# One LayerNorm group for token tiles 0 and 1, and a new task order ahead of the second FFN chunk

## The chip, the cores and the metric

The kernel runs on one core of one Trainium2 chip. The metric is the device time of one launch in microseconds (us), as the median of several runs. Its engines are TensorE (PE, whose weight loads have a row of their own, PEld), VectorE (DVE), ScalarE (ACT), GpSimd (POOL) and SyncE (SP), which issues nearly all the DMAs.

## The reference

One transformer block on 2048 tokens of width 512: linear attention with a softmax feature map, then a gated FFN, both with a LayerNorm that is modulated by a condition vector c. The shapes are in the comments.

```python
mod = (silu(c) @ w_mod)                 # 6 vectors of 512: sa, ca, ga, sb, cb, gb
h = layernorm(x) * (1 + ca) + sa        # 2048 x 512
q, k, v = h @ wqkv                      # 32 heads of 16
pq, pk = q @ w_phi, k @ w_phi           # per head, 16 x 16
phi = lambda p: concat(softmax(p), softmax(-p))   # 32 features per head
kv = phi(pk).T @ v;  z = sum over tokens of phi(pk)
o = (phi(pq) @ kv) / (phi(pq) @ z + 1e-6)
x = x + ga * (o @ wo)
h = layernorm(x) * (1 + cb) + sb
x = x + gb * ((sigmoid(h @ w_gate) * (h @ w_up)) @ w_down)   # F = 1376
```

## The kernel before

The 2048 tokens are 16 tiles of 128. The program is a graph of 1230 small tasks with names; the text ORDER lists them all in one line, and each task's instructions go to the queue of its engine in that order. A name may end in @A, @D or @P, which puts the task on ACT, DVE or POOL; without it the task goes to the first engine in its own list. Every engine works its queue strictly in order. Buffers of a class (eight PSUM banks, eight `xn` and so on) are given out along the same text. Nothing else sets the order.

The tasks, with their lines in the kernel before:

- `ld_*`: loads, issued by SP (L537 x, L545 half of the K weights, L542 a quarter of the modulation weights). `wqT*` (L669) are transposed loads of the Q weights.
- `c1 c2 c3` turn c into silu(c); `modc1.0` and `modc1.1` (L630) are the products with the modulation weights, `modc1c0` and `modc1c1` (L635 to L638) copy the results out, each for half of the four 128-wide slices of D.
- `tpw*` (PE, L661) transpose the K weights, `wTc*` (L664) copy them out, `fold1*` (L679) fold w_phi into them, `foldc1*` (L685) copy that out. `fold0*` does the same for Q.
- First LayerNorm, by groups of tiles (the list LG): `st1_t` (DVE, L702) statistics, `rs1_g` the reciprocal root (ACT L709 or POOL L712), `nmr1_g` (DVE, L718) minus mean times that, `xn1_t` (L727 ACT, L729 DVE, L731 POOL) the normalised tile, `tph` (PE, L744) its transpose, four tasks per group, and `hm1` (L751 ACT, L753 DVE and POOL), which copies out a transposed slice with the modulation. An hm1 of a group of two tiles is 256 wide, of one tile 128. Before, tiles 0 and 1 are groups of their own; the others are pairs.
- Keys of tile t: `Kt` (PE, L817, four matmuls of 512 columns, for tiles 0 to 7 in halves a and b), `et` (ACT, L776, exp of both signs), `nt` (DVE, L780, sums), `rt` (the reciprocal, DVE L798 or ACT L794 and L795), `phit` (L787, DVE or POOL). Values: `Vt` (PE, L821) and `vat` (ACT, L836, the copy). `kvt` (PE, L282) adds phi times v into two PSUM banks. Tile 11 is cut in four parts for this, tiles 13 to 15 in two.
- `kvz` and `kvn` (DVE, L299 and L294) copy the two finished sums out. Only then can any output begin.
- Queries: `Qt` (PE, L871), `qet`, `qnt`, `qphit.s` (L784), `pTt` (a transposing DMA, L874).
- Output of a tile: `num` (PE, L326), `rd` and `u` (DVE, L329 and L333, the division), `oT`, `out` (PE, L356), `x1` (DVE, L361), then the second LayerNorm (`st2`, `rs2`, `nmr2`, `xn2`, `xnT`, `mod`). `tsw` loads the table for tanh on ACT.
- FFN by chunks of 1, 1, 2, 4, 4 and 4 tiles: `g` and `u` (PE, L447), `tg` (ACT, L457), `hm` (DVE, L468), `y` (PE, L485), `fin` (DVE, L492), `st` (the store).
- `warm0` (six matmuls) and `warm1_0` to `warm1_11` (one each, PE, L600) multiply zeros from the last block of w_down. The load of that block's real rows, `ld_wd2`, waits for the last of them.

## Time and profile before

| | us |
|---|---|
| median of 3 runs | 203.33 |
| lowest, highest | 203.19, 203.52 |
| span of the profiled execution | 202.2 |
| PE busy in it | 194.4 (96%) |
| DVE busy | 160.6 (79%) |
| ACT busy | 105.3 (52%) |
| POOL busy | 104.2 (52%) |

The profiled execution's time is known only as this span, from its first to its last instruction. Busy shares are means over stages of very different kinds: the start until the first K, the stage of keys and values, and the long rest, in which the outputs and the FFN run. They are read stage by stage. A matmul's record in the trace is longer than the distance to the next, since matmuls are pipelined; prices are therefore taken from start to start.

### The profile page before, as it was taken

What the parts mean: (1) busy time and instruction counts of PE and PEld (TensorE: products, weight loads), DVE (VectorE), ACT (ScalarE), POOL (GpSimd) and SP (SyncE); (2) the same over time, 40 slices, a digit from 0 to 9 for tenths busy, and PEclk for the clock granted to TensorE, in tenths of its full rate; (3) what the DMA queues carried; (4) which work ended last, traced back from release to release, by engine and by line L of the source; (5) the groups of instructions that cost most, each with busy time, mean ns of one, the idle gap of its engine ahead of it and who ended that gap; (6) DMA issues with size and microseconds to landing.
All of it is one profiled execution on the core that took longest, in us unless ns stands there. A gap on an engine that the chain in (4) does not pass through costs nothing.

```text
span 202.2 us, 4128 instructions
## 1 busy us (share of the span) xinstructions
PE 194.4 (96%) x1447; PEld 106.2 (53%) x1471; DVE 160.6 (79%) x376; ACT 105.3 (52%) x250; POOL 104.2 (52%) x146
## 2 busy tenths in 40 slices
...
GB/s 169 329 262 239 289 232 111 114 71 261 396 254 77 133 109 51 82 39 108 117 79 80 53 79 85 100 104 52 26 26 81 2 78 54 28 5 26 28 54 57
DMA packets 49452, 22.92 MB, mean 113 GB/s; under 512 B 38065, under 2 KB 47634, under 8 KB 49426
## 3 DMA queue, kind: packets, MB, share of 16 engines
...
q8 instruction: 12, 0.20, 0.4%
...
HBM read 11.58 MB, written 2.10 MB: 68 GB/s over the span
## 4 chain that ended last, share of the span: by engine, by line
PE 70%; ACT 15%; DVE 8%; issue 2%; POOL 2%; DMA 1%; POOLq 0%; DVEq 0%
PE y_ps L485 19%; PE u_ps L447 18%; PE g_ps L447 18%; PE a_ps L356 5%; ACT h1T L751 3%; ACT e L776 3%; ACT qe L776 2%; PE num L326 2%; PE k_ps L817 2%; DVE qks L780 2%; ACT wqk_f L685 2%; PE v_ps L821 2%; DVE ks L780 1%; DMA x_sb<-in_A_x_dram 1%; DVE phi L787 1%
## 5 line engine op out<-in xcount | busy, mean ns | idle before, releaser
L457 ACT ACTIVATE tg<-g_ps 128x512 bf16<-128x512 f32 (+5 forms) x66 | 28.7, 455 | 66.8 <-PE g_ps L447 39.9
L468 DVE SCALAR_TENSOR_TENSOR wmod_sb<-tg,u_ps 128x512 bf16<-128x512 bf16 (+4 forms) x63 | 30.2, 491 | 18.0 <-ACT tg L457 11.5
L485 PE MATMUL y_ps<-wd_sb,wmod_sb 128*128 128x512 bf16 (+4 forms) x180 | 44.2, 366 | 0.2
L447 PEld LDWEIGHTS <-wg_sb 128*128 128x128 bf16 (+1 forms) x252 | 21.9, 99 | 16.1 <-issue 0.2
L447 PEld LDWEIGHTS <-wu_sb 128*128 128x128 bf16 (+1 forms) x252 | 21.7, 99 | 15.9 <-issue 0.3
L784 POOL TENSOR_TENSOR qphi<-qe,qks 128x512 bf16<-128x512 bf16 x24 | 25.1, 1064 | 4.1 <-DMA pT<-qphi 1.4
L485 PEld LDWEIGHTS <-wmod_sb 128*128 128x128 bf16 (+1 forms) x187 | 17.1, 98 | 16.0 <-issue 0.6
L447 PE MATMUL u_ps<-wT_sb,wu_sb 128*128 128x512 bf16 (+2 forms) x124 | 23.8, 322 | 0.1
L447 PE MATMUL g_ps<-wT_sb,wg_sb 128*128 128x512 bf16 (+2 forms) x122 | 23.0, 321 | 0.2
L447 PE MATMUL g_ps<-wqk_sb,wg_sb 128*128 128x128 bf16 (+4 forms) x127 | 19.9, 287 | 0.1
L447 PE MATMUL u_ps<-wqk_sb,wu_sb 128*128 128x128 bf16 (+4 forms) x127 | 19.8, 286 | 0.2
L780 DVE TENSOR_REDUCE ks<-e 128x64 f32<-128x1024 bf16 (+2 forms) x22 | 19.3, 904 | 0.2
L492 DVE TENSOR_TENSOR ot<-y_ps,x 128x512 bf16<-128x512 f32 (+2 forms) x17 | 11.1, 654 | 10.1 <-PE y_ps L485 10.1
L780 DVE TENSOR_REDUCE qks<-qe 128x64 bf16<-128x1024 bf16 x16 | 19.1, 1204 | 0.0
L376 POOL TENSOR_SCALAR ve<-mv 128x2 f32<-128x2 f32 (+1 forms) x8 | 1.8, 226 | 33.4 <-DVE mv L366 33.3
L776 ACT ACTIVATE e<-k_ps 128x512 bf16<-128x512 f32 (+2 forms) x44 | 18.3, 536 | 0.0
L776 ACT ACTIVATE qe<-q_ps 128x512 bf16<-128x512 f32 x32 | 17.1, 612 | 0.8 <-POOL phi L787 0.6
L787 POOL TENSOR_TENSOR phi<-e,kr 128x1024 bf16<-128x1024 bf16 (+2 forms) x10 | 14.9, 1501 | 2.5 <-DVE phi L787 1.2
L817 PE MATMUL k_ps<-wqk_f,h1T 128*128 128x512 bf16 x61 | 16.1, 379 | 0.1
L356 PE MATMUL a_ps<-wo_sb,oT 128*128 128x512 bf16 x60 | 15.9, 379 | 0.2
L871 PE MATMUL q_ps<-wqk_f,h1T 128*128 128x512 bf16 x61 | 15.7, 379 | 0.2
L821 PE MATMUL v_ps<-wv_sb,h1T 128*128 128x512 bf16 x61 | 15.3, 379 | 0.1
...
## 6 DMA issues: line engine op xcount, KB each, us to landing
...
```

The source lines that it names most:

```text
L356: pe.matmul(ap_[:], lhsT=oT[:, j, :], rhs=wo_sb[:, j, :], start=(j == 0), stop=(j == KT - 1))
L447: pe.matmul(ps[:fsz, 0:n], lhsT=w[:, j, ft * P:ft * P + fsz], rhs=h[:, j, 0:n], start=(j == 0), stop=(j == KT - 1))
L457: G.add(f"tg{k}.{ft}", {"ACT": 0.13 + n * 0.00083}, lambda e, tg=tg, g_ps=g_ps, fsz=fsz, n=n: act.activation(tg[:fsz, 0:n], g_ps[:fsz, 0:n ...
L468: dve.scalar_tensor_tensor(hm_all[:fsz, hm[k].slot, ft, 0:n], tg[:fsz, 0:n], 1.0, u_ps[:fsz, 0:n], op0=ALU.add, op1=ALU.mult)
L485: mm = pe.matmul(y[:, 0:c1 - c0], lhsT=hm_all[:fsz, hm[k].slot, ft, tl * P:(tl + 1) * P], rhs=wd_sb[:fsz, ft, c0:c1], start=(ft == 0), sto ...
L776: act.activation(ee[:, a:b, s].rearrange("p g f h -> p g (f h)"), kp[:, a * 64:b * 64].rearrange("p (g n) -> p g n", n=64), ACT.Exp, scale ...
L780: dve.tensor_reduce(ks[:, a:b].rearrange("p g s h -> p (g s) h"), ee[:, a:b].rearrange("p g s f h -> p (g s) h f"), axis=AX.X, op=ALU.add)
L784: engine(e).tensor_tensor(ph[:].rearrange("p (g s f h) -> p g s f h", s=2, f=DH, h=4)[:, :, s], ee[:, :, s], ks[:, :, 1 - s].unsqueeze(2). ...
L787: engine(e).tensor_tensor(ph[:, a * P:b * P].rearrange("p (g f h) -> p g f h", f=DH, h=4), ee[:, a:b].rearrange("p g s f h -> p (g s) f h" ...
L817: pe.matmul(kp[:], lhsT=h1T[:, j, t * P:(t + 1) * P], rhs=wqk_f[:, j, D:2 * D], start=(j == 0), stop=(j == KT - 1))
L821: pe.matmul(vp[:], lhsT=h1T[:, j, t * P:(t + 1) * P], rhs=wv_sb[:, j, :], start=(j == 0), stop=(j == KT - 1))
L871: pe.matmul(qp[:], lhsT=h1T[:, j, t * P:(t + 1) * P], rhs=wqk_f[:, j, 0:D], start=(j == 0), stop=(j == KT - 1))
```

## The change

The list LG is changed so that tiles 0 and 1 form one group, and TD (which groups are transposed by DMA) accordingly. Tile 0's `xn1` had been bound to DVE and now takes the common form, with an `nmr` of its own (list XP). The tasks rs1_1, nmr1_1 and the four tph and four hm1 of tile 1 alone are gone; the four hm1 of the group are 256 wide. Tasks of the first LayerNorm are now named by their group's first tile (rs1_8 is the group of tiles 8 and 9, before rs1_5). 1221 tasks are left.

ORDER is new up to the second FFN chunk, and some 45 tasks stand on other engines. From the second chunk on the order of the matmuls is the same. New switches come with it: HALF, QHALF, RPAIR are empty and ROWS and WPQ are 0, so that the code they guard makes no tasks. The tile `mone` is wider.

```diff
-LG = [[0], [1], [2, 3], [4, 5], [6, 7], [8, 9], [10, 11], [12, 13], [14, 15]]
-TD = [0, 0, 0, 0, 0, 0, 1, 1, 0]
+LG = [[0, 1], [2, 3], [4, 5], [6, 7], [8, 9], [10, 11], [12, 13], [14, 15]]
+TD = [0, 0, 0, 0, 0, 1, 1, 0]
...
+XP = [1, 2, 3, 4, 5, 6, 7, 8, 9, 10, 11, 12, 13, 14, 15, 0]
...
-        if g:
-            def f_nm(e, ts=ts):
-                for t in ts:
+        xp = [t for t in ts if t in XP]
+        if xp:
+            def f_nm(e, xp=xp):
+                for t in xp:
...
-            G.add(f"xn1_{t}", {"POOL": 0.69, "ACT": 0.73} if t else {"DVE": 0.3}, f_xn, r=[("rs1", g)] + ([("nmr1", g)] if t else []), w=[("xn1", t)],
+            G.add(f"xn1_{t}", {"POOL": 0.69, "ACT": 0.73, "DVE": 0.3} if t in XP else {"DVE": 0.3}, f_xn, r=[("rs1", g)] + ([("nmr1", g)] if t in XP else []), w=[("xn1", t)],
```

Two lines of ORDER in its new form, from the end of the keys stage; `warm1_8` to `warm1_11` had stood ahead of the first K:

```diff
+V13 warm1_8 warm1_9 Q3 r12.0 phi15.0@D phi12.0@D r15.4@A qn6.0 va13 kv12.0 kv13.0 kv13.4 va15 kv14.0 kv15.0 kvz0 kvn0 phi15.4 kv14.4 kv15.4 kvz1 kvn1 wo0 wo2
+wo3 qe3.0 qn3.0 qphi3.1@P qphi3.0@P Q7 qe7.0 num0a rd0a num0b rd0b Q15 num2b warm1_10 warm1_11 num1a num1b num4a num2a gwb grb ld_wu0 ld_wd ld_wg0 qphi6.0@P
```

The engines whose load moves, tile by tile:

- hm1 from DVE to ACT: 0.2, 6.0, 4.3, 8.0, 8.2, 14.1, 14.3 (14.x is the slice x of the group of tiles 14 and 15); from ACT to DVE: 2.1, 4.0, 6.3; of the two groups transposed by DMA, 10.1 from POOL to ACT, 12.1 from ACT to POOL, 12.0 from POOL to DVE.
- phi from DVE to POOL: 3, 4, 7, three quarters of 11 and a half of 13; from POOL to DVE: 6 and 8.
- r from DVE to ACT: 3, 6, 8 and a half of 14; from ACT to DVE: 4, 5, 9, 12.
- xn1_3 from ACT to POOL, xn1_0 from DVE to POOL, xn1_6 from POOL to DVE; rs1_8 from POOL to ACT; modc1c0, foldc02 and va2 from ACT to DVE.

Three places of the order, engine by engine. First ACT from the first reciprocal root (`rs_84`) to the first exp (`e`), before:

```order
L709 ACTIVATE ve_83<-mv_82,eps 128x1
L710 ACTIVATE rs_84<-ve_83 128x1
L727 ACTIVATE xn<-x_sb,nmr,rs_84 128x512
L664 COPY wT_sb<-tp_w 128x4x128 x4
L685 CAST wqk_f<-fold_ps 128x512 x3
L635 COPY modc<-modc_ps 128x2
L636 ACTIVATE modc<-modc_ps 128x2
L751 ACTIVATE h1T<-tp_h,modc 128x256
L751 ACTIVATE h1T<-tp_h,modc 128x128
L751 ACTIVATE h1T<-tp_h,modc 128x256
L751 ACTIVATE h1T<-tp_h,modc 128x128
L685 CAST wqk_f<-fold_ps 128x512
```

And the same place now:

```order
L740 ACTIVATE ve_83<-mv_82,eps 128x2
L741 ACTIVATE rs_84<-ve_83 128x2
L695 COPY wT_sb<-tp_w 128x4x128 x4
L716 CAST wqk_f<-fold_ps 128x512 x4
L783 ACTIVATE h1T<-tp_h,modc 128x256 x9
L810 ACTIVATE e<-k_ps 128x8x64 x2
```

The xn and the modc copies are gone from here, the wT copies come right behind the roots, and nine wide h1T stand in one run.

Second the loads that SP issues first, before:

```order
L537 DMA x_sb<-in_A_x_dram 128x2x512 x2
L545 DMA wqk_sb<-in_A_wqkv_dram 128x2x512
L537 DMA x_sb<-in_A_x_dram 128x2x512
L545 DMA wqk_sb<-in_A_wqkv_dram 128x2x512
L537 DMA x_sb<-in_A_x_dram 128x2x512
L542 DMA wmod_sb<-in_w_mod_dram 128x4x256 x2
L537 DMA x_sb<-in_A_x_dram 128x2x512
L542 DMA wmod_sb<-in_w_mod_dram 128x4x256 x2
L537 DMA x_sb<-in_A_x_dram 128x2x512
L669 DMA_TRANSPOSE wT_sb<-in_A_wqkv_dram 128x4x128
L537 DMA x_sb<-in_A_x_dram 128x4x512
L551 DMA wv_sb<-in_A_wqkv_dram 128x4x512
```

And now:

```order
L546 DMA x_sb<-in_A_x_dram 128x2x512 x3
L559 DMA wqk_sb<-in_A_wqkv_dram 128x2x512 x2
L546 DMA x_sb<-in_A_x_dram 128x2x512
L554 DMA wmod_sb<-in_w_mod_dram 128x4x256 x2
L546 DMA x_sb<-in_A_x_dram 128x2x512
L554 DMA wmod_sb<-in_w_mod_dram 128x4x256 x2
L546 DMA x_sb<-in_A_x_dram 128x2x512
L546 DMA x_sb<-in_A_x_dram 128x4x512
L565 DMA wv_sb<-in_A_wqkv_dram 128x4x512
L700 DMA_TRANSPOSE wT_sb<-in_A_wqkv_dram 128x4x128 x4
```

The first half of the K weights (`wqk_sb`) is now the fourth load instead of the third, tiles 0 and 1 come first (the rows don't tell tiles apart), and all transposed loads stand behind wv.

Third ACT at the end of the keys stage, from a full exp of a query (`qe`) to the next, before:

```order
L776 ACTIVATE qe<-q_ps 128x8x64 x2
L836 CAST vaug_110<-v_ps 128x32x16
L794 ACTIVATE ks<-ks 128x32
L795 ACTIVATE kr<-ks 128x32
L836 CAST vaug_113<-v_ps 128x32x16
L836 CAST vaug_111<-v_ps 128x32x16
L776 ACTIVATE qe<-q_ps 128x8x64 x4
```

And now:

```order
L877 CAST vaug_111<-v_ps 128x32x16
L877 CAST vaug_110<-v_ps 128x32x16
L810 ACTIVATE qe<-q_ps 128x8x64 x2
L833 ACTIVATE ks<-ks 128x32
L834 ACTIVATE kr<-ks 128x32
L877 CAST vaug_113<-v_ps 128x32x16
L877 CAST vaug_112<-v_ps 128x32x16
L810 ACTIVATE qe<-q_ps 128x8x64 x6
```

In both the last half reciprocal (`ks`, `kr`) is followed by two copies of values (`vaug`); now three more queries' exps come right behind, where before there were two.

More of the change, by code (lines that the diff above doesn't have):

```diff
@@ L35 @@
 DIRECT = [1, 0]
+HALF = []
+QHALF = []
+XP = [1, 2, 3, 4, 5, 6, 7, 8, 9, 10, 11, 12, 13, 14, 15, 0]
+RPAIR = []
+ROWS = 0
+WPQ = 0
 VSP = 4
@@ new lines @@
+rs1_6@P ld_wk0 warm1_6 tpw1 wTc1 tpw0 wTc0 ld_wk1 tpw3 wTc3 tpw2 wTc2 fold11 foldc11 fold13 foldc13 fold12 foldc12 tph0.0 fold10 foldc10 nmr1_2 xn1_2 xn1_3
+ld_x1a st1_5 c3 nmr1_6 xn1_7 st1_4 rs1_4@P ld_wm00a ld_wm00b modc1.0 tph0.2 modc1c0@D hm1_0.0@A tph0.1 tph2.2 hm1_0.1@A tph2.0 hm1_2.0@A xn1_6@D tph6.0
+hm1_6.0@A tph2.1 tph6.1 tph0.3 hm1_6.1@A ld_x2b st1_10 st1_11 rs1_10@P hm1_2.1 ld_wm01a ld_wm01b modc1.1 modc1c1@D hm1_0.3@A hm1_0.2@A K2a tph2.3 tph6.2
+hm1_6.2@A hm1_2.2@A nmr1_4 xn1_4 xn1_5 K3a K0a K0b e0.0 ld_x2a st1_8 st1_9 rs1_8 nmr1_10 xn1_11 xn1_10 K1a K1b hm1_2.3 K3b e3.0 K2b e2.0 e1.0 ld_x3a st1_14
@@ L234, with f_wp @@
     act.dma_start(c_row[:], c)
-    with nc.allow_non_contiguous_dma(reason="small w_phi load"):
-        act.dma_start(wp_sb[:], A_w_phi.rearrange("(kt hl) d f -> (hl d) kt f", hl=8))
+    def f_wp(e):
+        with nc.allow_non_contiguous_dma(reason="small w_phi load"):
+            e.dma_start(wp_sb[:], A_w_phi.rearrange("(kt hl) d f -> (hl d) kt f", hl=8))
+    if not WPQ:
+        f_wp(act)
     act.preload_act_table_set("natural_log_exp_and_others")
```

143 lines of the change are left out of this document (83 added, 60 removed).

## The prediction

> **What bounds the kernel now.** I read the page first, then the busy time by stage, then the chain that ended last, then the time lines of ScalarE (ACT), GpSimd (POOL), VectorE (DVE) and TensorE (PE). The stretch from the first key matmul to the first `num` matmul, with engines in the order PE, PE weight load, DVE, ACT, POOL:
>
> ```profile
> span 202.2 us, 4128 instructions
> core 0: us, PE busy (x) PEld busy (x) DVE busy (x) ACT busy (x) POOL busy (x), PEclk, DMA share, GB/s
> 0.00:5.00 5.00, 3.75 (x13) 1.25 (x14) 1.87 (x5) 1.44 (x2) 1.77 (x15) 1.00 0.59 167
> 13.20:57.38 44.18, 43.18 (x411) 24.28 (x416) 43.63 (x92) 43.07 (x117) 38.43 (x44) 1.00 0.89 225
> ```
>
> Between 13.2 and 57.4 us three engines are full at once: DVE 43.6, PE 43.2 and ACT 43.1 of 44.2 us. Only POOL has 5.8 us free. What the change shifts among engines therefore counts where the fullest of them ends. The edges of the stage, on PE:
>
> ```profile
> 1.25 2.74 PE L600 MATMUL warm<-wd_sb 128*128 128x512 bf16 x6 [1.25 <-DVE wd_sb L593]
> 4.12 2.74 PE L600 MATMUL warm<-wd_sb 128*128 128x512 bf16 x6
> 13.21 0.54 PE L630 MATMUL modc_ps<-sc_bf,wmod_sb 128*128 128x1 bf16 x16
> 13.62 0.38 PE L817 MATMUL k_ps<-wqk_f,h1T 128*128 128x512 bf16 x1
> 57.38 0.93 PE L326 MATMUL num<-kvb,pT 128*128 128x68 bf16 x24 [0.43 <-DVE kvb L294]
> 102.19 2.59 PE g_ps L447 x12
> ```
>
> The last row (the chain) gives PE's price: 2.59/12 = 0.216 us per 512-column matmul. After 57.4 PE stays nearly full to the end. The matmuls are the same set before and after, so the time moves by when PE's real work starts, by warm-up matmuls that fall into it, and by PE's waits.
>
> **The change part by part.** *Start.* The second quarter of the modulation weights is still the eleventh load in SP's queue, and `modc1.1` still stands ahead of the first K. It ran at 13.21 and took until 13.62. Beside it, DVE in the new order runs ten statistics ahead of `hm1_2.1`. Laid end to end, from 3.66 at 0.82 each (the first two rows below) and 1.7 us for c3, three nmr pairs, an xn and hm1_2.1 itself, this ends at about 13.55. I put the first K (K2a) at 13.65 instead of 13.62: no gain, +0.03.
>
> ```profile
> 3.66 0.69 DVE L702 BATCH_NORM_STATS2 st<-x_sb 128x6 f32<-128x512 bf16 x1 [1.93 <-DMA x_sb<-in_A_x_dram]
> 4.48 0.66 DVE L702 BATCH_NORM_STATS2 st<-x_sb 128x6 f32<-128x512 bf16 x1
> 7.19 0.69 DVE L702 BATCH_NORM_STATS2 st<-x_sb 128x6 f32<-128x512 bf16 x1 [0.22 <-DMA x_sb<-in_A_x_dram]
> 6.47 0.61 PEld L661 LDWEIGHTS <-wqk_sb 128*128 128x128 bf16 x6 [0.52 <-DMA wqk_sb<-in_A_wqkv_dram]
> 7.96 0.45 PEld L661 LDWEIGHTS <-wqk_sb 128*128 128x128 bf16 x8 [0.66 <-DMA wqk_sb<-in_A_wqkv_dram]
> ```
>
> *ACT's start.* The first half of the K weights moves from third to fourth load, behind tokens 6 and 7. The rows show the third landing at 6.45, the fourth at 7.18, the fifth at 7.95. So `tpw1` starts at about 7.2, and ACT's first copy of it near 7.65. Before, ACT came to it at 7.33, after its `xn1_3`, which now goes to POOL. ACT is full from there on, in both orders.
>
> ```profile
> 6.63 0.80 ACT L727 ACTIVATE xn<-x_sb,nmr,rs 128x512 bf16<-128x512 bf16 x1
> 7.33 2.14 ACT L664 COPY wT_sb<-tp_w 128x512 bf16<-128x512 bf16 x4
> 11.11 0.16 ACT L635 COPY modc<-modc_ps 128x2 f32<-128x2 f32 x1
> 11.37 2.11 ACT L751 ACTIVATE h1T<-tp_h,modc 128x256 bf16<-128x256 bf16 x4
> 5.46 0.29 ACT L709 ACTIVATE ve<-mv,eps 128x2 f32<-128x2 f32 x1 [1.08 <-DVE mv L703]
> 5.79 0.20 ACT L710 ACTIVATE rs<-ve 128x2 f32<-128x2 f32 x1
> 34.99 0.33 ACT L794 ACTIVATE ks<-ks 128x64 f32<-128x64 f32 x1
> 35.52 0.57 ACT L836 CAST vaug<-v_ps 128x512 bf16<-128x512 f32 x1
> 54.49 0.25 ACT L794 ACTIVATE ks<-ks 128x32 f32<-128x32 f32 x1
> 54.97 1.06 ACT L836 CAST vaug<-v_ps 128x512 bf16<-128x512 f32 x2
> 13.96 2.32 ACT h1T L751 x6
> 16.28 0.48 ACT wqk_f L685
> 16.75 0.47 ACT h1T L751
> ```
>
> *ACT's load from there to its last `va`.* From 7.33 to 56.03 (54.97 + 1.06) is 48.70 us. Prices, start to start: a 256-wide h1T 0.465; a 128-wide one 0.35 (2.32 for four of them and two wide); wqk_f 0.48, a vaug about the same; a reciprocal by logarithm 0.53 (34.99 to 35.52), its half 0.48 (54.49 to 54.97); rs 0.5; modc1c 0.26. Removed: six narrow h1T (-2.10), modc1c0 (-0.26), foldc02 and va2 (-0.96), one reciprocal (-0.53). Added: seven wide h1T (+3.26), since four of merged tiles 0 and 1 and three of others now stand here, rs1_8 (+0.50), one half reciprocal (+0.48). Net +0.39. ACT ends its last `va` at 7.65 + 48.70 + 0.39 = 56.7 instead of 56.0. This is the term that decides.
>
> *POOL and the end of the keys.* In both orders the last reciprocal on ACT stands 0.94 before its end, so now at 55.8, and POOL's last `phi` waits for it:
>
> ```profile
> 51.42 3.06 POOL L787 TENSOR_TENSOR phi<-e,kr 128x512 bf16<-128x512 bf16 x3 [1.18 <-DVE phi L787]
> 55.14 1.46 POOL L787 TENSOR_TENSOR phi<-e,kr 128x512 bf16<-128x512 bf16 x1 [0.66 <-ACT kr L795]
> 56.75 0.21 DVE L299 SCALAR_TENSOR_TENSOR kvb<-kvacc,mask 128x16 bf16<-128x16 f32 x1
> ```
>
> One such phi took 1.02 (3.06/3) or 1.46. I take the 1.46, which stood at this same place, so 57.2 and the last kv at about 57.3. Then come Q7 (4 x 0.216 = 0.86) and the first `num`, at 58.1 instead of 57.38: **+0.73**. With 1.02 it would be +0.3. The Trainium skill, SBUF — State Buffer, section Who interferes with whom, says that a VectorE instruction with two SBUF inputs and a GpSimd instruction that reads SBUF exclude each other, the later one blocking fully. By that rule the 1.46 was a phi held up by a DVE phi, and as DVE's last ones now run earlier, the 1.02 would hold. POOL as a whole takes on a full phi, three quarters and a half more, 4.5 halves at 1.02 = 4.6 us, with one xn more and two rs pairs less, and has 5.8 free: I cost that at nothing; where it isn't covered it is up to those 4.6.
>
> *From there to the end.* Five of the twelve warm-ups, all ahead of the first K before, now stand behind it, three before the first `num` (already in its time, since PE waits there anyway) and two after it: **+0.43**. Q5 moves behind, Q7 ahead, which cancels. DVE's first query reduction now stands ahead of the first `den`, but Q15 and the two warm-ups are about as long (1.3 us) as that wait. PE's waits later on are 1.0 us in all:
>
> ```profile
> 57.38:100.00 42.62, 42.11 (x441) 30.55 (x449) 39.93 (x112) 29.22 (x73) 36.42 (x43) 1.00 0.58 96
> 100.00:198.00 98.00, 97.47 (x508) 45.47 (x517) 66.71 (x142) 24.37 (x43) 20.50 (x32) 1.00 0.26 54
> ```
>
> Q13, moved into the first FFN chunk, and earlier `num3` tasks can fill part of them: **-0.4**, between 0 and -0.6. Hidden at no cost: the table load for tanh, moved behind the modulation of the first chunk, where ACT has slack; the transposed loads of wq, moved behind wv (needed by PE only at 20 us); the last rows of w_down, whose load must wait for the last warm-up at about 59, with oT2 and pT3 queued behind it on SP, first needed later. Lists HALF, QHALF, RPAIR are empty, ROWS and WPQ are 0: nothing.
>
> Sum: 0.03 lies inside the 0.73; 0.73 + 0.43 - 0.4 = +0.76. The profiled execution has no time of its own beside its span of 202.2, which would become 203.0; the median of the three runs is 203.33, 1.13 more, which I keep: **204.1 us**.
>
> **The rivals.** *PE bounds the keys stage, not ACT.* PE's work from K2a to the first `num` is the old 43.76 us, less at least 1.0 idle (44.18 - 43.18), plus 0.65 for three warm-ups, less 0.22 for four transposes of 128 columns (a quarter of 0.216 each) that now come earlier. From 13.65 that ends at 56.8; with half of the idle staying, 57.3. Then -0.1 + 0.43 - 0.3: 203.4. For it speaks that ACT's busy time includes stalls that a looser order need not have.
>
> *Faster: DVE decides, and it is relieved.* DVE is the fullest engine and stood without a gap before kvb.
>
> ```profile
> L753 DVE TENSOR_SCALAR h1T<-tp_h,modc 128x256 bf16<-128x256 bf16 x8 | 3.1, 401 | 0.0
> L753 DVE TENSOR_SCALAR h1T<-tp_h,modc 128x128 bf16<-128x128 bf16 x2 | 0.7, 336 | 0.0
> L787 DVE TENSOR_TENSOR phi<-e,kr 128x1024 bf16<-128x1024 bf16 x7 | 4.5, 673 | 0.0
> L787 DVE TENSOR_TENSOR phi<-e,kr 128x512 bf16<-128x512 bf16 x2 | 0.8, 432 | 0.0
> L787 DVE TENSOR_TENSOR phi<-e,kr 128x256 bf16<-128x256 bf16 x3 | 0.8, 295 | 0.0
> L798 DVE RECIPROCAL kr<-ks 128x64 bf16<-128x64 f32 x4 | 2.2, 538 | 0.0
> L361 DVE TENSOR_TENSOR x<-a_ps,x_sb 128x512 f32<-128x512 f32 x2 | 1.4, 681 | 0.0
> ```
>
> It loses two narrow h1T (-0.67), two wide (-0.80), a whole phi (-0.67), a half (-0.43), three quarters (-0.89), and gains a reciprocal (+0.54) and two copies out of PSUM, which the last row bounds (+1.36): -1.6, about -1.2 with the small instructions. kvb would come at 55.5, and PE's own 56.8 would bind: -0.6 + 0.43 - 0.4 = -0.57, 202.8. It decides if ACT's last `va` ends before 55.9, 0.8 ahead of my sum. Against it: the +0.39 of ACT is counted instruction by instruction.
>
> *Slower still: PE's rate.* The first warm-ups took 0.457 each (2.74/6), twice the later 0.216, though the granted clock reads 1.00 there. Between 7 and 13.6 us PE now has five warm-ups fewer. If the slow rate returned for as long as it lasted at the start (1.25 to 6.86, 5.6 us), PE would lose 2.8, of which its 1.3 us of waiting (58.1 - 56.8) hides part: 205.6. The Trainium skill, TensorE: Matmul & The Clock Gate, Part 1, has the array at half clock until a window of about 3.4 us is busy and again after an idle one; by an estimate from that page the loss would be 1.7 us before hiding, some 204.5. No wait of this length stands in PE's order, which speaks against it.
>
> **How the numbers follow.** ACT as summed: chance 0.48, 203.7 to 204.7. PE: 0.26, 203.1 to 203.8. DVE: 0.18, 202.4 to 203.0. PE's rate: 0.08. About 0.2% (0.41 us) is what measurements of this kernel can tell from no change. Faster: the DVE case and a rest of PE's, 0.19. Same: most of PE's and a little of the first, 0.27. Slower: 0.54. The range goes from 202.8, in the middle of the DVE case, to 205.2, short of the rate case: about 0.17 is left out. The likeliest case alone has 203.7 to 204.7.
>
> **What would show it.** Right: first K within 0.2 of 13.65; ACT without gaps from about 7.65 to a last `va` at 56.4 to 57.0; PE waiting for over 1 us in all between 50 and 57.5; the first `num` at 57.7 to 58.4. Wrong: a first `num` before 57.2, or K ahead of 13.3, or warm-ups standing in waits that PE would have had anyway. A K pitch above 0.3 would show the rate case.

## The result, and the profile after

The changed kernel takes 208.37 us (median of six runs, 207.41 to 209.77), the kernel before in the same session 203.43 (six runs, 203.19 to 204.33). The ratio is 1.0238, 95% interval 1.0201 to 1.0275. The forecast was 204.1 with a range to 205.2; the sign was right, the time 3.2 us beyond the range.

The six times fall into two groups, and each run's mean granted clock of TensorE tells them apart: 207.41, 207.48 and 207.71 at a clock of 1.00, and 209.03, 209.31 and 209.77 at 0.992, 0.992 and 0.984. The profiled execution, 209.03 with a span of 206.9, is of the second group. Single executions of a_wk0, a_qn and the kernel before that took 229 to 291 us at a mean clock of 0.66 to 0.85 are left out of all figures. The clock row of the page (40 equal slices of the span, in tenths of full speed) and the busy time by stage (engines in the order PE, PE weight load, DVE, ACT, POOL, then the granted clock) show where it is lost:

```profile
PEclk9978999999999999999999999999999999999999
```

```profile
core 0: us, PE busy (x) PEld busy (x) DVE busy (x) ACT busy (x) POOL busy (x), PEclk, DMA share, GB/s
11.00:13.00 2.00, 1.46 (x26) 1.01 (x23) 1.93 (x7) 1.99 (x6) 1.92 (x4) 1.00 1.14 323
13.50:16.00 2.50, 2.50 (x10) 1.11 (x10) 2.43 (x11) 2.38 (x5) 2.38 (x4) 0.50 1.27 314
16.00:17.00 1.00, 1.00 (x5) 0.37 (x4) 0.96 (x4) 0.00 (x0) 0.93 (x3) 0.68 1.18 245
17.00:19.00 2.00, 2.00 (x16) 1.05 (x15) 1.11 (x6) 1.85 (x5) 1.58 (x3) 1.00 1.51 85
...
13.25:59.31 46.06, 45.21 (x404) 24.32 (x401) 44.45 (x87) 43.43 (x117) 41.98 (x45) 0.96 0.85 206
```

From 13.5 to 16 us, just as the key matmuls begin, the clock is halved. The stage from the first K to the first `num` takes 46.06 us where it took 57.38 - 13.62 = 43.76. PE's time line, in the places that the prediction named and near the end (start, duration, what ran, the idle time before it and who ended that):

```profile
9.11 0.88 PE L710 MATMUL fold_ps<-bd,wT_sb 128*128 128x128 bf16 x8 [0.58 <-ACT wT_sb L695]
13.25 1.15 PE L858 MATMUL k_ps<-wqk_f,h1T 128*128 128x512 bf16 x2
14.62 4.20 PE L858 MATMUL k_ps<-wqk_f,h1T 128*128 128x512 bf16 x14
18.65 0.50 PE L776 MATMUL tp_h<-ident,xn 128*128 128x128 bf16 x6
57.40 1.21 PE L291 MATMUL kvacc<-vaug,phi 128*128 128x68 bf16 x32 [0.80 <-DVE phi L826]
59.31 0.42 PE L335 MATMUL num<-kvb,pT 128*128 128x68 bf16 x8
167.60 0.19 PE L528 MATMUL bnd<-bst,ones_f 128*1 128x3 f32 x2
167.73 2.55 PE L494 MATMUL y_ps<-wd_sb,wmod_sb 128*128 128x512 bf16 x11
171.79 2.76 PE L494 MATMUL y_ps<-wd_sb,wmod_sb 96*128 96x512 bf16 x12 [1.52 <-DVE flag L534]
174.39 1.89 PE L456 MATMUL u_ps<-wT_sb,wu_sb 128*128 128x512 bf16 x8
```

Two things stand there that the kernel before did not have. Fourteen K matmuls took 18.65 - 14.62 = 4.03 us, 0.288 each against 0.216. And at 171.79 PE had waited 1.52 us for a flag. That flag is the last of a chain of small tasks near the end (`bnd*`, `ldf`), which the first part of this document did not describe, because the change was not seen to touch it. A matmul (`bndc`, L528) and four small DVE instructions (`bndd`, L531 to L534) compute a bound on the data. `ldf` then loads the flag into registers of PE, ACT and POOL, for a branch behind the last task. The first matmul that names the value is `y14.0`, late in the last chunk, but `ldf` itself stands in PE's queue, and PE cannot pass it. DVE's time line shows why the flag was late:

```profile
169.02 0.69 DVE L501 TENSOR_TENSOR ot<-y_ps,x 128x512 bf16<-128x512 f32 x1 [1.98 <-PE y_ps L494]
169.63 0.62 DVE L431 TENSOR_SCALAR wT_sb<-wT_sb,modc 128x256 bf16<-128x256 bf16 x1
170.16 0.14 DVE L531 COPY bs<-bnd 1x3 f32<-1x3 f32 x1
170.92 0.14 DVE L534 TENSOR_SCALAR flag<-bs 1x1 int32<-1x1 f32 x1
```

DVE takes up `bndd` only behind `fin10` (L501, which waits for y matmuls) and `mod71` (L431). The flag is written at 171.06, and PE goes on 0.73 us later. In ORDER, `ldf` had stood behind a good part of the last chunk's matmuls; the change put it right behind `bndd`, so that only 11 y matmuls lay between the matmul `bndc` and `ldf`. In the kernel before, the y matmuls behind `bndc` (there L519) ran through to the next `u`, 5.11 us later, where it is now 174.39 - 167.60 = 6.79:

```profile
164.67 0.19 PE L519 MATMUL bnd<-bst,ones_f 128*1 128x3 f32 x2
164.80 5.15 PE L485 MATMUL y_ps<-wd_sb,wmod_sb 128*128 128x512 bf16 x23
169.78 1.89 PE L447 MATMUL u_ps<-wT_sb,wu_sb 128*128 128x512 bf16 x8
```

The milestones of ACT and POOL in the changed kernel, first ACT, then POOL:

```profile
7.52 2.03 ACT L695 COPY wT_sb<-tp_w 128x512 bf16<-128x512 bf16 x4
11.51 4.37 ACT L783 ACTIVATE h1T<-tp_h,modc 128x256 bf16<-128x256 bf16 x9
17.12 1.08 ACT L810 ACTIVATE e<-k_ps 128x512 bf16<-128x512 f32 x2 [1.24 <-PE k_ps L858]
56.68 1.06 ACT L877 CAST vaug<-v_ps 128x512 bf16<-128x512 f32 x2
```

```profile
56.91 1.34 POOL L826 TENSOR_TENSOR phi<-e,kr 128x512 bf16<-128x512 bf16 x1 [0.54 <-ACT kr L834]
```

ACT was without gaps from 7.52, as forecast, until the halved K matmuls made it wait 1.24 us at 17.12.

For all that follows the program is cut at four events on PE's time line: the first `num`; the first `g` matmul of 256 columns (the chunk of two tiles); the matmul `bndc`; the first `u` matmul behind it. From the first 256-wide `g` to `bndc` every profiled execution below took 76.13 to 76.16 us, and from that `u` to the end of DVE's last instruction 29.26 to 29.27. What follows DVE's last instruction, the last store among it, took 2.7 to 3.8 us (before 3.15, after 3.24). So nearly the whole difference lies in three stretches. In microseconds:

| kernel | mean clock | first num | num to g | bndc to u | span |
|---|---|---|---|---|---|
| before | 0.998 | 57.38 | 31.14 | 5.11 | 202.2 |
| after | 0.992 | 59.31 | 32.16 | 6.79 | 206.9 |
| difference | | +1.93 | +1.02 | +1.68 | +4.7 |

### The profile page after: what moved, and what is told of

It is laid out like the page before. It is cut to its first block, busy times and chain, and to the rows that moved or that the text cites. A ratio compares the mean times of both kernels' runs of the same rounds, so it can differ in the third digit from the quotient of the medians.

```text
span 206.9 us, 4151 instructions
## 1 busy us (share of the span) xinstructions
PE 197.9 (96%) x1471; PEld 106.6 (52%) x1471; DVE 161.1 (78%) x370; ACT 105.6 (51%) x249; POOL 107.8 (52%) x147
## 4 chain that ended last, share of the span: by engine, by line
PE 67%; DVE 2%; ACT 1%; issue 1%; POOL 0%; POOLq 0%
PE y_ps L494 18%; PE u_ps L456 17%; PE g_ps L456 17%; PE a_ps L365 6%; PE q_ps L912 4%; PE num L335 2%; PE g_ps L458 1%; PE u_ps L461 1%; ACT L396 1%; PE kvacc L291 1%; ACT wqk_sb L435 1%; DVE phi L826 0%; DVE wT_sb L431 0%; POOL wqk_sb L433 0%; PE tpo L354 0%
## 5 line engine op out<-in xcount | busy, mean ns | idle before, releaser
L494 PE MATMUL y_ps<-wd_sb,wmod_sb 128*128 128x512 bf16 (+4 forms) x187 | 45.6, 366 | 1.5 <-DVE flag L534 1.5
L826 POOL TENSOR_TENSOR phi<-e,kr 128x1024 bf16<-128x1024 bf16 (+2 forms) x15 | 19.8, 1333 | 2.8 <-DVE vaug L877 1.3
L501 DVE TENSOR_TENSOR ot<-y_ps,x 128x512 bf16<-128x512 f32 (+2 forms) x17 | 11.1, 653 | 11.9 <-PE y_ps L494 11.8
L858 PE MATMUL k_ps<-wqk_f,h1T 128*128 128x512 bf16 x64 | 17.9, 404 | 0.0
L912 PE MATMUL q_ps<-wqk_f,h1T 128*128 128x512 bf16 x64 | 16.3, 379 | 0.0
L862 PE MATMUL v_ps<-wv_sb,h1T 128*128 128x512 bf16 x64 | 15.8, 379 | 0.0
```

Of the source, the lines that this page charges most:

```text
L494: mm = pe.matmul(y[:, 0:c1 - c0], lhsT=hm_all[:fsz, hm[k].slot, ft, tl * P:(tl + 1) * P], rhs=wd_sb[:fsz, ft, c0:c1], start=(ft == 0), sto ...
L826: engine(e).tensor_tensor(ph[:, a * P:b * P].rearrange("p (g f h) -> p g f h", f=DH, h=4), ee[:, a:b].rearrange("p g s f h -> p (g s) f h" ...
L858: pe.matmul(kp[:], lhsT=h1T[:, j, t * P:(t + 1) * P], rhs=wqk_f[:, j, D:2 * D], start=(j == 0), stop=(j == KT - 1))
L862: pe.matmul(vp[:], lhsT=h1T[:, j, t * P:(t + 1) * P], rhs=wv_sb[:, j, :], start=(j == 0), stop=(j == KT - 1))
L912: pe.matmul(qp[:], lhsT=h1T[:, j, t * P:(t + 1) * P], rhs=wqk_f[:, j, 0:D], start=(j == 0), stop=(j == KT - 1))
```

## The experiments

The theories to be told apart: the halved clock comes from the warm-ups that the change took away ahead of K (A); the flag's wait is a cost of its own (B); and what is left belongs to the new order of the start or of the outputs (C). All results first; each kernel was timed against the kernel before on the same chip. "Low" is the share of its runs with a mean clock under 0.993.

| run | median us | ratio, 95% interval | low | first num | num to g | bndc to u |
|---|---|---|---|---|---|---|
| after | 208.37 | 1.0238 [1.0201, 1.0275] | 3 of 6 | 59.31 | 32.16 | 6.79 |
| a_ldf | 206.56 | 1.0147 [1.0118, 1.0176] | 2 of 6 | 58.39 | 32.24 | 5.11 |
| a_warm | 206.64 | 1.0150 [1.0130, 1.0169] | 0 of 4 | 58.08 | 31.87 | 6.81 |
| a_both | 205.27 | 1.0085 [1.0070, 1.0101] | 0 of 6 | 57.60 | 32.06 | 5.11 |
| b_ldf | 203.80 | 1.0014 [1.0004, 1.0023] | 0 of 12 | 57.16 | 31.14 | 5.27 |
| a_drop | 207.77 | 1.0196 [1.0155, 1.0237] | 3 of 6 | 59.60 | 32.41 | 6.80 |
| b_drop | 204.17 | 1.0040 [1.0020, 1.0060] | 7 of 8 | 57.56 | 31.14 | 5.11 |
| a_ldf5 | 206.11 | 1.0108 [1.0083, 1.0133] | 0 of 6 | 57.72 | 32.48 | 5.73 |
| h_newstart | 204.85 | 1.0067 [1.0052, 1.0083] | 0 of 6 | 57.71 | 31.14 | 5.11 |
| h_newrest | 204.95 | 1.0077 [1.0052, 1.0103] | 0 of 6 | 57.37 | 32.81 | 5.11 |
| h_q5 | 204.67 | 1.0046 [1.0028, 1.0065] | 1 of 12 | 57.33 | 31.36 | 5.11 |
| h_q57 | 204.92 | 1.0060 [1.0039, 1.0080] | 0 of 8 | 57.77 | 31.26 | 5.11 |
| b_q7 | 203.80 | 1.0005 [0.9986, 1.0025] | 0 of 12 | 57.33 | 31.16 | 5.11 |
| a_wk0 | 205.36 | 1.0101 [1.0078, 1.0123] | 0 of 5 | 57.64 | 32.25 | 5.10 |
| a_qn | 208.09 | 1.0192 [1.0165, 1.0220] | 2 of 6 | 57.69 | 35.77 | 5.11 |
| m_merge | 206.44 | 1.0127 [1.0097, 1.0156] | 6 of 6 | 60.65 | 31.22 | 5.11 |
| m_merge2 | 204.26 | 1.0033 [1.0014, 1.0052] | 4 of 12 | 58.04 | 31.24 | 5.11 |

### The flag's load put back (a_ldf)

```diff
-mod81@P fin10 y8.7 y8.8 mod83@P y9.1 mod71 y9.2 st10 y8.9 mod80@P bndd ldf y8.10 y9.3
+mod81@P fin10 y8.7 y8.8 mod83@P y9.1 mod71 y9.2 st10 y8.9 mod80@P bndd y8.10 y9.3
...
-hm5.9 u5.5 tg5.0 u5.8 hm5.0 g5.5 tg5.8
+hm5.9 u5.5 tg5.0 u5.8 hm5.0 ldf g5.5 tg5.8
```

> The changed kernel, with one task moved: the load of the flag into registers (ldf) stands behind the first g5.1 columns of the last chunk again, ahead of g5.5, as before the change, instead of right behind bndd. Theory: in the changed kernel TensorE waited 1.52 us for the flag at 171.79, with eleven y matmuls of work done 1.5 us earlier and nothing to take their place; that wait goes, so the time falls by 1.4 to 1.7 us, the median from 208.4 to about 206.8, and the idle time of TensorE between 164 and 175 us from 1.5 to under 0.1. Rival: the wait only stood in for others (of y matmuls for the two PSUM banks that VectorE's fin frees); then another wait of over 1 us shows there and the time falls by less than 0.5. Either way about half of the runs still show a mean clock below 1.00, since the start is unchanged.

It fell by 1.8 us, but from three low runs in six to two. The same edit between a_warm and a_both, neither of which had a low run, is worth 206.64 - 205.27 = 1.37, just under the 1.4 to 1.7 expected. The same place on PE's time line:

```profile
166.76 0.19 PE L528 MATMUL bnd<-bst,ones_f 128*1 128x3 f32 x2
166.89 5.15 PE L494 MATMUL y_ps<-wd_sb,wmod_sb 128*128 128x512 bf16 x23
171.87 1.89 PE L456 MATMUL u_ps<-wT_sb,wu_sb 128*128 128x512 bf16 x8
```

All 23 y matmuls run through, and the stretch is the 5.11 us of before. No other wait took the flag's place; theory B holds.

### The warm-ups put back (a_warm), and both (a_both)

```diff
-rs1_6@P ld_wk0 warm1_6 tpw1
+rs1_6@P ld_wk0 warm1_6 warm1_7 tpw1
...
-modc1.0 tph0.2
+modc1.0 warm1_8 warm1_9 tph0.2
...
-tph2.2 hm1_0.1@A tph2.0
+tph2.2 warm1_10 hm1_0.1@A tph2.0 warm1_11
...
-V11 warm1_7 K14
+V11 K14
...
-V13 warm1_8 warm1_9 Q3
+V13 Q3
...
-Q15 num2b warm1_10 warm1_11 num1a
+Q15 num2b num1a
```

> The changed kernel, with warm1_7 to warm1_11 back ahead of the first K: one behind warm1_6, two behind modc1.0, two among the transposes of the second group. Theory A (the granted clock): with TensorE thinly used from 7 to 13 us the clock falls to 0.50 for about 3 us at K's start in half of the runs; with the five matmuls back it does not, all runs show a mean clock of 1.00, and the K pitch is 0.22 everywhere. Then the median is the 207.5 of the changed kernel's runs at full clock, less 0.4 to 0.6 for the two or three warm-ups that TensorE had no wait to hide: 206.9 to 207.1. Theory B (the lower clock has nothing to do with these five matmuls): the mean clock is again 0.98 to 0.99 in some of the runs, and the median 207.5 to 208.4.

> Both edits of the two runs above. If the two causes are all that was not foreseen, what is left is the forecast without its two late warm-ups: 204.1 - 0.43 = 203.7, with the first num at 57.7 to 58.2 (the forecast's ACT term of +0.7, its three earlier warm-ups being gone too). If the extra 0.6 us that the trace shows between the first num and the second chunk is a cost of its own, 204.2 to 204.6. If the keys stage is bound by TensorE or VectorE instead of ACT, the first num comes at 57.3 or earlier and the time is 203.4 or less.

With the five matmuls ahead of K no run showed a low clock, and a_warm's median came out a little below theory A's figure. With both edits 205.27 is left, 3.1 us less than the changed kernel but 0.7 above the 204.2 to 204.6 that were expected for a third cost: 1.75 us over the 203.52 of before that it was timed against. K runs at full rate again (first fence PE, then ACT, then POOL, all of a_both):

```profile
13.15 0.73 PE L858 MATMUL k_ps<-wqk_f,h1T 128*128 128x512 bf16 x2
14.02 3.18 PE L858 MATMUL k_ps<-wqk_f,h1T 128*128 128x512 bf16 x14
17.04 0.50 PE L776 MATMUL tp_h<-ident,xn 128*128 128x128 bf16 x6
55.69 1.21 PE L291 MATMUL kvacc<-vaug,phi 128*128 128x68 bf16 x32 [1.24 <-DVE phi L826]
57.60 0.42 PE L335 MATMUL num<-kvb,pT 128*128 128x68 bf16 x8
59.40 0.62 PE L354 MATMUL tpo<-ident,o 128*128 128x128 bf16 x4
60.11 1.02 PE L912 MATMUL q_ps<-wqk_f,h1T 128*128 128x512 bf16 x4
```

```profile
7.58 2.05 ACT L695 COPY wT_sb<-tp_w 128x512 bf16<-128x512 bf16 x4 [0.26 <-PE tp_w L692]
54.96 1.06 ACT L877 CAST vaug<-v_ps 128x512 bf16<-128x512 f32 x2
```

```profile
55.19 1.35 POOL L826 TENSOR_TENSOR phi<-e,kr 128x512 bf16<-128x512 bf16 x1 [0.53 <-ACT kr L834]
```

Fourteen K matmuls take 17.04 - 14.02 = 3.02 us, 0.216 each. The other rows are used further below.

### The warm-ups taken away altogether, after (a_drop) and before (b_drop)

```diff
-    for i in range(12):
+    for i in range(7):
         warm(f"warm1_{i}", 1, 0.22, r=["c1"], w=["warm"])
```

The five names are gone from ORDER, too.

> The changed kernel without its five late warm-ups (warm1_7 to warm1_11 exist no more; the load of the last rows of w_down then waits for warm1_6 alone). It leaves out five multiplications of zeros and nothing of the result. TensorE between 7 and 13 us is as thinly used as in the changed kernel. If the lower clock at K's start comes from that thin use, it must still come in about half of the runs: mean clock 0.98 to 0.99 there, 208 to 209 us, and 206.6 in the others (207.5 less up to 1.08 for five matmuls of 0.216). If it came from the late warm-ups' place in any other way, or is chance, all runs have a mean clock of at least 0.997 and the median is about 206.6, as in the run with the five ahead of the first K.

> The kernel before without warm1_7 to warm1_11, five multiplications of zeros that stand ahead of the first K (nothing of the result is left out). If these five are what keeps the granted clock up at K's start, whatever the rest of the order, then the clock falls to 0.5 there in a good part of the runs: mean clock 0.98 to 0.99, and 204.5 to 205.5 in those runs. If it is rather the new order's longer runs of transposes of 128 columns that let it fall, all runs keep a mean clock of at least 0.997 and the time stays at 203.3 to 203.8.

a_drop still has the low clock in three of six runs, so it is not the late place of the warm-ups that brings it. b_drop is the sharper test, since all of the old order stays: without the five it has the low clock in seven of eight runs. Its busy time by stage, in the columns of the first such table:

```profile
11.00:13.00 2.00, 1.59 (x22) 1.08 (x22) 1.97 (x8) 1.97 (x8) 1.78 (x4) 0.73 1.25 272
13.00:15.00 2.00, 1.78 (x15) 0.90 (x14) 1.77 (x8) 1.79 (x5) 1.92 (x4) 0.50 1.07 320
15.00:17.00 2.00, 2.00 (x17) 1.26 (x16) 1.93 (x8) 1.84 (x5) 1.85 (x4) 0.91 1.18 326
```

Counted over the kernels of the table that keep the starts of before or after: with the five ahead of K and no long wait of PE, 1 run of 77 had a low clock (a_warm, a_both, b_ldf, a_ldf5, the four h kernels, b_q7, a_wk0); without them 15 of 26 (after, a_ldf, a_drop, b_drop). In over 60 runs of the kernel before that were timed beside them, one was low (204.87 at 0.992). Theory A is shown. The five do not keep the clock up whatever else happens: in the two m kernels further below, which have them, PE stands still for 2.85 and 1.54 us ahead of K, and 10 of 18 runs are low. The old order bears it better: b_drop is 0.4% slower, while in the changed kernel the runs at a low clock are 209.37 - 207.53 = 1.84 us slower than the others (means of three).

### How late the flag may be asked for: before with early ldf (b_ldf), and a middle place (a_ldf5)

```diff
-y9.5 y9.6 y11.7 bndd y9.7 y9.8
+y9.5 y9.6 y11.7 bndd ldf y9.7 y9.8
...
-st8 ldf g5.5
+st8 g5.5
```

> The kernel before, with one task moved: ldf right behind bndd, as the change has it. Theory: this alone costs the 1.4 to 1.7 us that the changed kernel's trace shows as a wait for the flag, 203.4 to about 204.9, a wait of TensorE of 1.3 us or more on the flag at about 167 us. Rival: in the old order bndd comes early enough, or other matmuls stand behind ldf's user, so that less than 0.4 us shows.

The rival was right here: only 0.28 us (0.14%). In the old order 17 y matmuls lie between `bndc` and `bndd`, against 11 in the new. So the place behind `bndd` is not bad in itself; it is bad with `bndd` that early. The middle place tests that, on a_warm:

```diff
-y8.9 mod80@P bndd ldf y8.10 y9.3 y9.4 y9.5 y9.6 y11.7
+y8.9 mod80@P bndd y8.10 y9.3 y9.4 y9.5 y9.6 ldf y11.7
```

> The kernel with the warm-ups ahead of K (206.64 with ldf 11 y matmuls behind bndc, wait 1.53 us), with ldf five y matmuls later, so 16 behind bndc. Theory: the flag arrives a fixed time after bndc, 11 x 0.216 + 1.5 = 3.9 us, since VectorE first ends fin10 and mod71; each y matmul that stands ahead of ldf instead of behind it takes 0.216 off the wait. So the wait becomes 1.53 - 5 x 0.216 = 0.45 us and the time 206.64 - 1.08 = 205.56. Rival: the wait is a cost of the register load itself, wherever it stands; then it stays near 1.5 us, and the time at 206.6.

```profile
166.34 0.19 PE L528 MATMUL bnd<-bst,ones_f 128*1 128x3 f32 x2
166.47 3.63 PE L494 MATMUL y_ps<-wd_sb,wmod_sb 128*128 128x512 bf16 x16
170.56 1.68 PE L494 MATMUL y_ps<-wd_sb,wmod_sb 128*128 128x512 bf16 x7 [0.46 <-issue]
```

The wait is 0.46, as worked out. PE passes `ldf` 170.56 - 166.34 = 4.22 us after `bndc`, and in the changed kernel 171.79 - 167.60 = 4.19: a fixed time, which takes some 19 y matmuls to cover. The time fell less than expected, to 206.11. The ratios step down, 1.0150, 1.0108, 1.0085 with 11, 16 and all 23 matmuls in between, but the intervals of neighbours overlap; it is the stretch from `bndc` to `u` that tells the steps apart: 6.81, 5.73, 5.11.

### Start or outputs: two hybrids (h_newstart, h_newrest)

Up to `kvn1`, the last copy of the finished sums, one hybrid has the order and engines of a_both, and behind it those of before; the other has it the other way round, with Q5 and Q7 exchanged. As a sketch of ORDER:

```diff
-[a_both up to kvn1] [a_both from there on]
+[a_both up to kvn1] [before from there on]
...
-[before up to kvn1] [before from there on]
+[before up to kvn1] [a_both from there on, Q5 and Q7 exchanged]
```

> A hybrid: the changed kernel with warm-ups ahead of K up to the two copies of the finished sums (kvn1), and from there on every task that is left in the order and on the engines of the kernel before (with its late ldf). It tells where the 1.75 us go that the kernel with both edits still loses. From the two traces, 0.44 us of it lie ahead of the first num and about 1.0 behind it (tile 0's transposes 0.5, a wait for the gate's tanh 0.1 to 0.4, y matmuls behind wd 0.2). If so, this hybrid is slower than before by about 0.4: 203.9 to 204.2 at a before of 203.5, ratio 1.002 to 1.003. Rival: the new start is itself the loss, and the stretch behind num only carries it on; then the ratio is 1.006 or more.

> The other hybrid: the kernel before up to kvn1, and the rest in the order and on the engines of the changed kernel, with late ldf and no warm-up left for it (all twelve stand ahead of K, as before); Q5 and Q7 change places there, since Q5 is done. If the loss behind the first num belongs to the new order of the outputs, this is slower than before by about 1.0 us, ratio 1.004 to 1.006. If it was only carried on from the start, the ratio is within 0.998 and 1.002.

Both ratios are higher than their theories had them. The new order of the outputs costs 1.0077 by itself (1.004 to 1.006 expected), and the table shows it where it was expected: 32.81 instead of 31.14 us from `num` to `g`, the first `num` unchanged. The new start costs 1.0067 where 1.002 to 1.003 was expected. That is the rival's figure, but the rival's reason, that the stretch behind `num` carries the loss on, does not hold: that stretch is 31.14 again in h_newstart, to the hundredth. The two do not add up, since together (a_both) they cost 1.0085.

Where the new start's loss lies can be read against b_ldf, whose profiled execution took 203.51 against 204.83, 1.32 less. The first `num` comes 0.55 later (57.71 against 57.16), the flag costs 0.16 less, what follows DVE's last instruction takes 0.71 longer (from 199.38 to 202.8 against 198.99 to 201.7), and the time outside the span is about 0.2 longer (204.83 - 202.8 = 2.0 against 203.51 - 201.7 = 1.8). Why the end behind DVE takes longer there stays open; it varies between profiles (3.03 in a_both, which has the same start, and 3.15 in the kernel before).

### Filling the waits at the end of the keys (h_q5, h_q57, b_q7)

```diff
-va13 kv12.0 kv13.0
+va13 Q5 kv12.0 kv13.0
...
-ld_wu0 grb Q5 ld_wg0
+ld_wu0 grb ld_wg0
```

h_q57 and b_q7 (this one on the kernel before) also move Q7:

```diff
-kv14.4 kv15.4 kvz1 kvn1 num0a num1a
+kv14.4 kv15.4 kvz1 kvn1 Q7 num0a num1a
...
-qe3.0 u0a
+qe3.0 qe7.0 u0a
```

> The hybrid with the new start (204.85), with Q5 moved from behind the last kv to ahead of kv12, where TensorE waits 1.24 us for a phi with nothing to do; before, Q5 stood there too. Theory: TensorE's empty wait there is what the new start costs at its end; Q5 (0.86) fits in it, but the first num then has to wait 0.4 for the copies as before. Net gain 0.4 to 0.5: first num at 57.2 to 57.4, time 204.3 to 204.5. Rival: the loss of this hybrid lies ahead of that (in K's start or VectorE's queue): then the last phi comes later by what Q5 delays, and the time stays at 204.7 to 205.0.

> As the run above, and Q7 ahead of the first num, so that both waits at the end of the keys are filled (1.24 and 0.42 us by 0.86 each). Theory: a further 0.4, 203.9 to 204.1; with that the new start would be within 0.6 of before. Rival: as above, 204.3 or more.

> The kernel before, with the query product Q7 moved ahead of the first num, as the change has it (its exp behind qe3.0). Before, TensorE waits 0.42 us there for the first copy of the finished sums. Theory: Q7 (0.86) fills that wait; the first num starts 0.44 later but 0.86 of work is done, so the time falls by 0.4: 203.0 to 203.1 at a before of 203.46. Rival: the exp of Q7 on ACT then stands ahead of the copy of tile 0's transposed output, and TensorE loses the 0.4 there: 203.4 to 203.6.

Q5 in PE's wait of 1.24 us brought the new start from 1.0067 to 1.0046 (the intervals overlap), and the first `num` to 57.33. Its 204.67 lies between the theory's 204.3 to 204.5 and the rival's 204.7 to 205.0, so the gain is not settled. Q7 ahead of `num`, the one part of the change that looked like a gain, brought nothing, neither there (1.0060) nor in the kernel before (1.0005). The row from b_q7 shows why; 0.43 us of waiting for `kvb` before `num` has become 0.41 behind it:

```profile
57.33 0.93 PE L326 MATMUL num<-kvb,pT 128*128 128x68 bf16 x24
58.66 1.02 PE L871 MATMUL q_ps<-wqk_f,h1T 128*128 128x512 bf16 x4 [0.41 <-ACT qe L776]
```

PE now waits for ACT to read an earlier query instead.

### ACT's start (a_wk0)

```diff
-ld_x1b st1_7 st1_6 rs1_6@P ld_wk0 warm1_6
+ld_wk0 ld_x1b st1_7 st1_6 rs1_6@P warm1_6
```

> The kernel with both edits (205.27), with the first half of the K weights loaded third again, ahead of tokens 6 and 7. ACT's first copy of it then starts at 7.2 to 7.3 instead of 7.58. If ACT's queue sets the end of the keys, as the forecast had it, ACT's last va and the first num come 0.3 earlier, time about 205.0. If VectorE sets it (it is the fullest, 43.84 of 44.45 us), tokens 6 and 7 coming 0.7 later hold up its statistics, and the first num comes no earlier or up to 0.3 later: 205.2 to 205.6.

Its ACT began the copies at 7.40 instead of a_both's 7.58, 0.18 earlier where 0.3 was meant. Its last `va` ended at 56.05 (a_both 56.02), the first `num` came at 57.64 (57.60), and the time did not fall. This speaks against ACT's start as what sets the end of the keys, but 0.18 us is too little to settle it.

### A sum on DVE put behind the division (a_qn)

```diff
-qe3.0 qn3.0 qphi3.1@P qphi3.0@P Q7
+qe3.0 Q7
...
-qe15.0 u0b tpo0
+qe15.0 u0b qn3.0 qphi3.1@P qphi3.0@P tpo0
```

> The kernel with both edits (late ldf, warm-ups ahead of K: 205.27), and VectorE's sum for the exp of query tile 3 (qn3.0, 1.21 us) moved from ahead of the first den to behind tile 0's division, its two qphi with it. Theory: there TensorE loses 0.49 us at the transposes of tile 0's output (rows at 59.40 and 60.11 where four transposes take 0.22), because the division stands behind this sum; the loss goes, 204.8 to 204.9. Rival: the transposed query tile 3 then comes later than the num that reads it at about 64.6 us, and TensorE waits there instead; then 205.2 to 205.6.

The rival, and far beyond its price:

```profile
59.45 0.38 PE L354 MATMUL tpo<-ident,o 128*128 128x128 bf16 x4
60.20 1.02 PE L912 MATMUL q_ps<-wqk_f,h1T 128*128 128x512 bf16 x4 [0.37 <-ACT qe L810]
...
68.50 0.43 PE L335 MATMUL num<-kvb,pT 128*128 128x68 bf16 x8 [2.56 <-DMA pT<-qphi]
```

From tile 0's transposes to the next matmul it is still 60.20 - 59.45 = 0.75 us (0.71 in a_both), since PE now waits there for ACT, and the `num` that needs query tile 3 waits 2.56 us for its transposed load. In two of six runs the clock was low; in the profiled one (209.1) it fell behind this wait, at 69 us.

### The merging alone (m_merge, m_merge2)

```diff
-LG = [[0], [1], [2, 3], [4, 5], [6, 7], [8, 9], [10, 11], [12, 13], [14, 15]]
+LG = [[0, 1], [2, 3], [4, 5], [6, 7], [8, 9], [10, 11], [12, 13], [14, 15]]
...
-st1_3 st1_2 st1_1 ld_x1b rs1_2 rs1_1
+st1_3 st1_2 st1_1 ld_x1b rs1_2
...
-ld_wm00b st1_0 tpw3 xn1_1
+ld_wm00b st1_0 rs1_0 nmr1_0 tpw3 xn1_1
```

m_merge2 has the group's start further ahead:

```diff
-st1_3 st1_2 st1_1 ld_x1b rs1_2 nmr1_2
+st1_3 st1_2 st1_1 st1_0 ld_x1b rs1_2 rs1_0 nmr1_2 nmr1_0 xn1_1 xn1_0
...
-ld_wm00b st1_0 rs1_0 nmr1_0 tpw3 xn1_1 xn1_2
+ld_wm00b tpw3 xn1_2
```

> The merging alone: tiles 0 and 1 are one group, all else stands in the order and on the engines of the kernel before; tile 0's xn stays on VectorE without an nmr, the reciprocal root of the group (one, on ACT) stands behind tile 0's statistics, and the four transposes and hm1 of the group stand where tile 0's stood. Theory (the merging is small, the new order costs): six fewer instructions on ACT and VectorE than before, 0.1 to 0.2 us each, against a first group that is ready later by tile 0's statistics: 203.2 to 203.9, first num 57.0 to 57.5, clock 1.00, no wait for the flag. Rival (the merging itself makes the start late): the first K over 0.4 us later than 13.6 and the time over 204.2.

> The merging alone again, in the order of the kernel before, but with the group's start put forward: tile 0's statistics right behind tile 1's, the root of the merged group where tile 1's stood, then nmr and the two xn. The first try lost 2.85 us at 8.3 us because GpSimd's xn waited for a root that stood behind ACT's copies of the K weights. Theory (the merging itself is small): first K at 13.4 to 14.0, full clock, 203.3 to 204.0. Rival (a group of two is ready later, whatever the order): the first K over 0.4 us later than 13.6, a wait of TensorE for an xn or hm1 of over 0.4 us ahead of it, and 204.2 or more.

The first is a failed try: PE stood still for 2.85 us for an xn that waited for the root, K began at 16.76, and the clock was low in every run. The second has K at 14.56, 0.9 later than before, and a smaller hole (its PE):

```profile
9.82 0.51 PE L776 MATMUL tp_h<-ident,xn 128*128 128x128 bf16 x6 [1.54 <-POOL xn L763]
```

It is 0.33% slower (0.14 to 0.52), and its eight runs at a full clock alone (median 204.1) are slower than before, too. The rival holds as far as this hole goes: in this place a group of two is ready later, and in the old order PE has nothing else to do. How much of K's delay is the hole is not shown, since this profile is one of the four low ones, with the clock halved from about 11.5 to 15 us, between the hole and K. Nor is it shown that the merging must cost that much in any order; in the new order the first K is on time.

## Why the prediction was wrong, step by step

The sign came out, partly by luck, since most of the time came from causes that the sum did not have. Of its terms, the 0.73 to the first `num` is near when the clock is undisturbed. What failed: the register load of the flag, which had no term and cost about 1.4 us; the rate of PE, held to be unlikely, which cost 1.84 us in half of the runs; and the -0.4 for the outputs, which cost about 1.0 instead.

**First K at 13.65, no gain.** The 13.25 of this profile is ahead of 13.3, which the prediction had named as a sign that it is wrong. That there is no clear gain holds all the same: the first K comes at 13.15 to 13.70 in the other profiles with this start, and at 13.09 to 13.62 with the old one.

**ACT's start and load.** Right in size. ACT's first copy came at 7.52 (7.65 forecast). With the clock undisturbed, in a_ldf, which is the same program up to the first `num`, ACT needed 48.90 us from its first copy to the end of its last `va`, against the 49.09 of the sum:

```profile
7.90 2.05 ACT L695 COPY wT_sb<-tp_w 128x512 bf16<-128x512 bf16 x4 [0.43 <-PE tp_w L692]
55.74 1.06 ACT L877 CAST vaug<-v_ps 128x512 bf16<-128x512 f32 x2
```

That this is "the term that decides" is not shown: a_wk0 speaks against it.

**POOL's last phi, first num at 58.1.** Near: 58.39 in a_ldf (K at 13.70). The sum took 1.46 for the phi; it took 1.34 in the changed kernel and 1.35 in a_ldf and a_both. The 1.02 that the prediction worked out beside the sum did not come, since DVE's last phi again ran beside it, where the prediction had it run earlier. PE was idle for 0.81 us between 50 and 57.5, in the changed kernel and in a_ldf, where over 1 us was named as the sign. In a_both:

```profile
54.68 0.96 DVE L826 TENSOR_TENSOR phi<-e,kr 128x512 bf16<-128x512 bf16 x2
55.55 1.21 DVE L819 TENSOR_REDUCE qks<-qe 128x64 bf16<-128x1024 bf16 x1
```

DVE begins its next instruction at 55.55, 0.36 after POOL's phi was begun at 55.19; 1.35 - 0.36 = 0.99. In the changed kernel the same sum gives 1.34 - (57.26 - 56.91) = 0.99, in the kernel before 1.46 - (55.62 - 55.14) = 0.98. The rule of the Trainium skill that the prediction weighed (SBUF — State Buffer, Who interferes with whom: two SBUF inputs on VectorE shut out a reading GpSimd) agrees with these rows; the premise of its use was off.

**"No wait of this length stands in PE's order, which speaks against it."** This step failed: the rate rival had a chance of 0.08, and its mechanism happened, in half of the runs. No long wait is needed. In the changed kernel PE's longest idle time between 7 and 13 us is 0.58 us, and still the clock fell; five matmuls of 512 columns decide it. The prediction's sign for it, a K pitch above 0.3, would have missed it: the fourteen K took 0.288 each on average, since the clock was back for the last of them. The price was too high (2.8 us of matmul time lost, where K's fourteen lost 1.01 and the first two and the transposes 0.5 more), and little of it was covered by PE's later waiting, because ACT waits for K as well (1.24 us at 17.12). Held against a_ldf's 58.39, the 59.31 puts the cost at 0.9, with K 0.45 earlier: 1.4; by the times it is 1.84.

**Warm-ups: 0.43, three of five hidden.** Not settled. a_ldf's three runs at a clock of 1.00 (206.19, 206.48, 206.63) stand 1.16 over a_both's median, about five times 0.216; a fourth, at 0.997, took the same 205.27 as a_both. And a_drop, which has none of the five anywhere, took 206.90, 206.98 and 207.52 at 1.00, on average only 0.4 less than the changed kernel's 207.53, though on a chip where the kernel before takes 203.77 instead of 203.43.

**"Q13, moved into the first FFN chunk, and earlier num3 tasks can fill part of them: -0.4".** Wrong in sign. From `num` to `g` the change costs 1.02, and 0.92 without any warm-up there (a_both). The rows of a_both above show a large piece, 0.49: four transposes of tile 0's output (`tpo`), 0.22 of work, hold PE for 60.11 - 59.40 = 0.71, because DVE's query sum stands ahead of the division. The prediction saw that sum and covered it with Q15 and the two warm-ups; in the changed kernel they do cover it, at their own price. h_newrest shows that the loss belongs to this order. Which of its waits could be mended singly is open, and the one try (a_qn) failed.

**"From there to the end".** The sum had no term for the last 40 us, on the ground that the order of the matmuls is the same from the second chunk on. It is; but a register load is no matmul, and it moved past twelve matmuls and more on PE's own queue. That was 1.68 us of the profile, the largest single error there, and that `ldf` had moved could be read from the order alone.

**The level.** The 1.13 us that the prediction kept between span and median came from two different executions. In every profile with a known time it is 1.7 to 2.2. The forecast difference does not hang on it.

The profile's 4.7 us are thus: 1.93 to the first `num` (forecast 0.73; the rest is nearly all clock), 1.02 to the `g` (forecast 0.03), 1.68 for the flag (not forecast).
